# A chunked attention with an 8-expert layer behind it: q and k of six blocks loaded as two tokens per row, and the routing's sums moved to another engine

## The chip, the cores and the metric

One core of a Trainium2 chip. The metric is the device time of one execution in microseconds (us).

## What is computed

From q, k and v of shape (4 batches, 8 heads, 768 tokens, 64), 8 memory keys and values per batch and head, gate weights (512 x 8) and expert weights w1 (8 x 512 x 1024) and w2 (8 x 1024 x 512), all fp32:

```python
for c in range(768 // 32):                     # chunks of 32 queries
    k_ctx = k[:, :, max(0, 32*c - 16) : min(768, 32*c + 40)]   # 16 left, 8 right; v alike
    s = q_c @ concat(mem_k, k_ctx).T / 8
    a = exp(s - max(s)); out_c = (a / (sum(a) + 1e-9)) @ concat(mem_v, v_ctx)
x = out as (3072 tokens, 512)
P = exp(x @ w_gate - max)
for _ in range(8):                             # the routing
    P /= P.sum(1, keepdims=True) + 1e-9
    P /= P.sum(0, keepdims=True) + 1e-9
    P *= 3072 / 8
y = sum over the experts e of P[:, e:e+1] * (relu(x @ w1[e]) @ w2[e])
```

## The kernel before

All 8 experts work on all 3072 tokens, in units of 512 tokens (six per expert, 48 in all). Each fp32 operand of a large product is split into two f16 parts, high and low, and a product is three passes of TensorE over the parts (high x high, high x low, low x high). From the second expert on the products use a seven-product form of 2x2 blocks, with sums of operands formed ahead; the first expert's outputs use the plain form.

**Attention** runs in 24 blocks of 128 tokens, four to a unit, and is spread over the first units. For block n, `load_block` (L834) loads q as 128 tokens x 8 heads x 64 (256-byte runs in memory, L850) and k likewise, shifted left by 16 tokens (L844, L845, L847). `load_extra` (kx, L784 to L792) loads the k rows between blocks and the memory keys, once for four blocks. `transposed` turns q and k, two heads at a time, by products with the identity (tiles tq, L1008, and tk, L1012: four transposes 128x128 each; tx, L808, for kx), and ACT copies them into qT (L1036) and kC (L1016 to L1029). Scores go to sp (L1071, 64 small products), DVE takes maxima and differences (sm L1085, s L1091), ACT the exponent, PE turns it (ta, L1128), and the values' product is xp (L1138). DVE scales it (rec, xq) and turns it into xg. Values are loaded by L923, one piece of 56 KB at a time, on SP's queue and, for block 0, on ACT's too.

**Scales.** Before a tensor is split it is scaled by a power of two found from its largest element. For x of the first unit: vmax of blocks 0 and 1 (DVE, L976), most_of (L445), a product row_x (L494) that lays the 128 maxima in a row, a maximum, a product sp_x (L481) that spreads it, and ux and sx on DVE (L456, L457). For the first weights alike: mxs (L557), row_w, sp_w, uw and sw. Then ACT makes the high part and DVE the low part of x and w (L513, L521), and the first expert's first products start (pp, L2040).

**Routing** (L1458 to L1545) starts when all logits (lg, 128 x 24 x 8) are there, beside the fifth and sixth units of the first expert. Each of 8 iterations has on DVE a row sum rs (L1494), its reciprocal (L1495, L1496), the scaling of lg (L1497) and a column sum cs (L1501); on PE cp, a product with ones (L1529), which adds over the partitions; on DVE cr (L1510, L1511) and the scaling of lg (L1512).

**Low parts.** In a unit's hidden part, L1821 subtracts the high from the full sum (h<-ss,h, 128x1024). It runs on POOL for units n < `ASIDE` (1) and on DVE for the others. POOL otherwise forms weight sums (ws, L601), operand sums (xt) and collects outputs (acc, L1926).

**What sets the order.** Every step is given to a planner (class Plan, L85 to L240) with an engine, a cost, the steps it needs and a due time. It lays them out in time and emits each engine's instructions in that order; the engines then run in that order, each waiting only for what its next instruction needs. Due times hang on START and TURN (the planned start and length of the first unit), UNIT (36.7, the others), `begin(n)` and `needed(n)` (when block n's result is due). Where PE has over 0.4 us to wait by the plan, `pad` puts in fillers, tile warm (L427), products with the identity that nobody reads, a count worked out from the gap:

```python
n = int((at - now - 0.1) * 0.8 / 0.11)
```

Of the kernel before, what the change touches and what calls it, by code (L numbers as in the profile page):

```python
# [233 lines left out]
def tile_chunked_attn_sinkhorn_moe(  # L234
# [28 lines left out]
    P = 128  # L263
# [29 lines left out]
    small = ctx.enter_context(tc.tile_pool(name="small", bufs=1))  # L293
    xpool = ctx.enter_context(tc.tile_pool(name="xpool", bufs=1))
# [51 lines left out]
    START, TURN, UNIT, AHEAD = 28.2, 63.0, 36.7, 50.0  # L346
# [3 lines left out]
    ASIDE = 1  # L350
# [388 lines left out]
    def needed(n):  # L739

        if n < BU:
            return (11.0, 17.5, 36.0, 41.0)[n]
        return PACE + ((n + 1) / BU - 1.0) * AHEAD - 12.1

    state = {}
    extra = {}
# [86 lines left out]

    def load_block(n):  # L834
# [4 lines left out]
        qt = buf("q", att, [P, H, D], F32, f"q_{n}")  # L839
        kt = buf("k", att, [P, H, D], F32, f"k_{n}")  # L840

        def go_k():
            if blk == 0:
# [5 lines left out]
        lq = add(  # L849
            "SP", 1, lambda: nc.sync.dma_start(qt.t, rows(q, b, t0, QB)), (), at, [qt], dma=1.55  # L850
        )
        lk = add("SP", 2 if blk == 0 else 1, go_k, (), at + 0.1, [kt], dma=1.55)
# [142 lines left out]
    def transposed(n):  # L995
# [10 lines left out]
        def go_q():  # L1006
            for i in range(HP):
                nc.tensor.transpose(tq.t[:, i], flat(qt, i), ident)  # L1008

        def go_k():  # L1010
            for i in range(HP):
# [19 lines left out]
        t = add("PE", 0.5, go_q, [lq], at, [qt, qT], takes=tq)  # L1031
# [11 lines left out]
        t = add("PE", 0.5, go_k, [lk], at, [kt, kC], takes=tk)  # L1043
# [413 lines left out]

    def routing(deps):  # L1458
# [4 lines left out]
        urgent = begin(LATE) + 58.5  # L1463
# [27 lines left out]
        def rows(it):  # L1491
            def go():
                rs = small.tile([P, NT], F32, tag="rs", bufs=1, name=f"rs_{it}")
                nc.vector.tensor_reduce(rs, lg, axis=AX.X, op=ALU.add)  # L1494
                nc.vector.tensor_scalar_add(rs, rs, 1e-9)  # L1495
                nc.vector.reciprocal(rs, rs)  # L1496
                nc.vector.tensor_tensor(  # L1497
                    lg, lg, rs[:, :, None].broadcast_to([P, NT, E]), op=ALU.mult
                )
                box[it] = small.tile([P, E], F32, tag="cs", bufs=1, name=f"cs_{it}")  # L1500
                nc.vector.tensor_reduce(  # L1501
                    box[it], lg.rearrange("p t e -> p e t"), axis=AX.X, op=ALU.add
                )
# [3 lines left out]
        def columns(it, cp):  # L1507
            def go():
                cr = small.tile([P, E], F32, tag="cr", bufs=1, name=f"cr_{it}")
                nc.vector.tensor_scalar_add(cr, cp.t, 1e-9)  # L1510
                nc.vector.reciprocal(cr, cr)  # L1511
                nc.vector.scalar_tensor_tensor(  # L1512
                    lg,
                    lg,
                    float(N) / float(E),
                    cr[:, None, :].broadcast_to([P, NT, E]),
                    op0=ALU.mult,
                    op1=ALU.mult,
                )

            return go

        for it in range(8):
            t = add("DVE", 1.8, rows(it), [t], urgent)
# [3 lines left out]
                0.4,  # L1528
                lambda it=it, cp=cp: nc.tensor.matmul(  # L1529
                    cp.t, ones, box[it], start=True, stop=True  # L1530
                ),
                [t],
                urgent,
                takes=cp,
            )
            t = add("DVE", 0.8, columns(it, cp), [t], urgent, frees=cp)
# [786 lines left out]
```

## Time and profile before

| | us |
|---|---|
| median of 3 runs | 1913.08 (1911.89 to 1914.97) |
| the profiled execution | 1913.3 |
| its span | 1911.5 |
| PE busy in the span | 1898.8 (99%) |
| DVE, ACT, POOL busy | 1468.1, 1022.5, 503.0 |
| mean granted clock of TensorE | 0.999 of full |

The profile follows one execution. Starts are counted from the span's start. PE is the multiplication of TensorE and PEld its weight load; DVE is VectorE, ACT ScalarE, POOL GpSimd, SP the engine that issues most DMAs. A timeline row covers neighbouring instructions of one kind; what stands in brackets is the engine's idle time before it and what ended that. The granted clock is 1.00 at 2.4 GHz and 0.50 at 1.2 GHz.

### The profile page before, as it was taken

How to read it: one execution, taken by the hardware profiler on the slowest of the kernel's cores; microseconds unless marked ns; L12 is line 12 of the kernel's file. 1: busy time of each engine (PE TensorE's matmuls, PEld its weight loads, DVE VectorE, ACT ScalarE, POOL GpSimd, SP SyncE). 2: the span in 40 equal slices, each digit the busy share in tenths (PEclk: the TensorE clock that was granted, in tenths of full speed). 3: DMA queues.
4: the chain of work that ended last, by engine and by line, in shares of the span. 5: the costliest groups of instructions: out<-in, count | busy, mean ns of one | idle time of the engine just before them, and what ended most of it. 6: DMA issues, size and time to landing. Idle time of an engine off the chain costs nothing.

```text
span 1911.5 us, 47024 instructions
## 1 busy us (share of the span) xinstructions
PE 1898.8 (99%) x19535; PEld 1634.8 (86%) x19535; DVE 1468.1 (77%) x2456; ACT 1022.5 (53%) x1999; POOL 503.0 (26%) x541
## 2 busy tenths in 40 slices
PE   8999999999999999999999999999999999999999
PEld 7777676788888888888888888888888888888888
DVE  5887679878589867898668875898678885786565
ACT  4665555556465545546446544655555563564453
POOL 1210012514134211522224231342124232332112
PEclk9999999999999999999999999999999999999999
DMA  8787653543324432264224433245313632222321
GB/s 198 189 219 182 160 173 133 169 169 106 126 80 160 150 134 77 90 217 165 84 91 154 165 119 114 84 155 188 127 45 111 247 112 97 98 84 83 127 84 67
DMA packets 212998, 254.81 MB, mean 133 GB/s; under 512 B 112240, under 2 KB 146480, under 8 KB 208432
## 3 DMA queue, kind: packets, MB, share of 16 engines
q1 hardware_dynamic: 210660, 251.21, 40.4%
q8 instruction: 153, 2.51, 0.6%
q10 hardware_dynamic: 2124, 0.59, 0.2%
q14 instruction: 61, 0.50, 0.1%
HBM read 187.84 MB, written 63.44 MB: 131 GB/s over the span
## 4 chain that ended last, share of the span: by engine, by line
PE 97%; DVE 2%; SPq 0%; ACT 0%; issue 0%; DMA 0%; POOL 0%; DVEq 0%; POOLq 0%
PE px L1593 26%; PE yx L1593 23%; PE pz L1593 13%; PE yz L1593 11%; PE py L1593 6%; PE yp L2121 6%; PE yy L1593 6%; PE pp L2040 1%; PE xp L1138 1%; PE sp L1071 1%; PE warm L427 1%; DVE w L521 1%; PE ta L1128 1%; PE tk L1012 1%; PE tq L1008 1%; SPq L923 0%
## 5 line engine op out<-in xcount | busy, mean ns | idle before, releaser
L1593 PEld LDWEIGHTS <-w 128*128 128x128 f16 x7896 | 771.2, 98 | 94.4 <-issue 2.8
L1593 PEld LDWEIGHTS <-h 128*128 128x128 f16 x7056 | 690.4, 98 | 81.1 <-issue 0.9
L1593 PE MATMUL px<-x,w 128*128 128x256 f16 x4512 | 547.8, 273 | 1.5 <-DVE c L1662 1.0
L1926 POOL TENSOR_TENSOR acc<-acc,y 128x256 f32<-128x256 f32 x252 | 262.4, 1049 | 881.1 <-ACT y L1901 868.5
L1593 PE MATMUL yx<-w,h 128*128 128x256 f16 x4032 | 467.9, 273 | 0.5 <-DVE acc L1936 0.5
L1652 ACT ACTIVATE q<-px 128x256 f32<-128x256 f32 x376 | 143.1, 382 | 289.6 <-PE px L1593 285.1
L1593 PE MATMUL pz<-x,w 128*128 128x256 f16 x2256 | 278.1, 273 | 0.0
L1593 PE MATMUL yz<-w,h 128*128 128x256 f16 x2016 | 233.8, 273 | 0.0
L1821 DVE TENSOR_TENSOR h<-ss,h 128x1024 f16<-128x1024 f32 x168 | 217.6, 1298 | 3.3 <-ACT h L1797 3.3
L1772 ACT ACTIVATE h<-c 128x768 f16<-128x768 f32 x168 | 140.7, 838 | 112.2 <-DVE c L1662 112.2
L1797 ACT CAST h<-ss 128x1024 f16<-128x1024 f32 x168 | 174.2, 1040 | 39.5 <-DVE ss L1761 39.5
L1761 DVE SCALAR_TENSOR_TENSOR ss<-c,ss 128x256 f32<-128x256 f32 x336 | 176.6, 525 | 8.6
L1805 DVE SCALAR_TENSOR_TENSOR h<-c,h 128x768 f16<-128x768 f32 x168 | 168.7, 1007 | 9.2 <-ACT h L1772 9.1
L1662 DVE SCALAR_TENSOR_TENSOR c<-px,q 128x256 f32<-128x256 f32 x188 | 77.8, 421 | 94.8 <-PE px L1593 85.6
L1901 ACT ACTIVATE y<-yx,pscale 128x256 f32<-128x256 f32 x168 | 79.6, 474 | 120.5 <-PE yx L1593 116.5
L1593 PE MATMUL py<-x,w 128*128 128x256 f16 x1128 | 139.0, 273 | 0.0
L2121 PE MATMUL yp<-w,h 128*128 128x512 f16 x576 | 132.0, 379 | 0.9 <-DVE h L2082 0.9
L1761 DVE SCALAR_TENSOR_TENSOR ss<-c,h 128x512 f32<-128x512 f32 x168 | 125.6, 748 | 1.9 <-ACT h L1749 1.9
L1662 DVE SCALAR_TENSOR_TENSOR c<-py,q 128x256 f32<-128x256 f32 x188 | 78.5, 421 | 62.0 <-PE py L1593 58.7
L1593 PE MATMUL yy<-w,h 128*128 128x256 f16 x1008 | 116.9, 273 | 0.0
L2121 PEld LDWEIGHTS <-h 128*128 128x128 f16 x576 | 55.3, 99 | 60.0 <-DVE h L2082 1.4
L513 ACT ACTIVATE w<-ws,sw 128x1024 f16<-128x1024 f32 (+1 forms) x64 | 69.5, 1090 | 65.7 <-POOL ws L601 65.6
(155 smaller groups left out, 1739.6 us busy)
## 6 DMA issues: line engine op xcount, KB each, us to landing
x<-xkeep SPq DMA_DIRECT2D x28, 1792.0 KB
akeep<-acc SPq DMA_DIRECT2D x168, 256.0 KB
acc<-akeep SPq DMA_DIRECT2D x168, 256.0 KB
w1f<-in_moe_w_dram SPq DMA_DIRECT2D x36, 512.0 KB
w2f<-in_moe_w_dram SPq DMA_DIRECT2D x32, 512.0 KB
w1fm<-in_moe_w_dram SPq DMA_DIRECT2D x28, 512.0 KB
w2fm<-in_moe_w_dram SPq DMA_DIRECT2D x28, 512.0 KB
xkeep<-x SPq DMA_DIRECT2D x6, 1792.0 KB
```

The source lines that it names most:

```text
L513: lambda: nc.scalar.activation(dst(0), src(), AF.Copy, scale=s),
L1593: nc.tensor.matmul(dst.t, a, b, start=(not more and n == 0), stop=(n == end), skip_group_check=more,)
L1652: lambda: nc.scalar.activation(t.t, src.t, AF.Copy, scale=DOWN),
L1662: lambda: nc.vector.scalar_tensor_tensor(c.t[:, o], src.t, DOWN, q.t, op0=ALU.mult, op1=ALU.add),
L1761: lambda: nc.vector.scalar_tensor_tensor(dst(), src(), 0.0, other(), op0=ALU.max, op1=op),
L1772: lambda: nc.scalar.activation(h.t[:, 0, 0:3], c.t, AF.Relu),
L1797: lambda: nc.scalar.copy(h.t[:, 0, 3:7], ss.t),
L1805: lambda: nc.vector.scalar_tensor_tensor(h.t[:, 1, 0:3].rearrange("p a n -> p (a n)"), c.t.rearrange("p a n -> p (a n)"), 0.0, h.t[:, 0, 0 ...
L1821: lambda: spare.tensor_tensor(h.t[:, 1, 3:7], ss.t, h.t[:, 0, 3:7], op=ALU.subtract),
L1901: (lambda: nc.scalar.activation(t.t, src.t, AF.Copy, scale=f))
L1926: lambda: nc.gpsimd.tensor_tensor(acc.t[:, cols], acc.t[:, cols], q.t, op=ALU.add),
L2121: nc.tensor.matmul(py.t, hf.t[:, hl, where[fh], o : o + P], room(fp, WIDE * wl + DM * fh, WIDE * wl + DM * (fh + 1)), start=(fp == 0 and i ...
```

## The change

- **Rows of two tokens.** q and k of blocks 0 to 5 are loaded as 64 partitions x 8 heads x 128, with 512-byte runs, into one half of a room of 128 partitions (block n in half n % 2). From block 6 on they are loaded as before, into the same rooms; block 6 waits until block 5 is turned.
- **Turned by products.** `two_turns` replaces the four transposes of such a block by 16 products 64x64 with the identity, whose results go to every second column of tq or tk.
- **Routing.** The row sums, the scaling by rows, the column sums and the scaling by columns go to POOL, as chains of two-operand sums in a new tile, tree. DVE keeps the reciprocals. The step is due earlier (begin(LATE) + 30.0, not 58.5).
- **ASIDE** goes from 1 to NU + 2 = 8: the eight L1821 subtractions of the first two units with the seven-product form go from DVE to POOL.
- **Plan times** (START, TURN and the due times of a unit's rebuilding, of weights and of maxima) become other numbers.

```diff
-    START, TURN, UNIT, AHEAD = 28.2, 63.0, 36.7, 50.0
+    START, TURN, UNIT, AHEAD = 30.0, 66.0, 36.7, 50.0
...
-    ASIDE = 1
+    ASIDE = NU + 2
...
+    def twos(src, b, t, m):
+
+        return src[b, :, t : t + m].rearrange("h (p a) d -> p h (a d)", a=2)
+
+    def two_turns(to, t, n):
+
+        r = slice(n % 2 * HB, (n % 2 + 1) * HB)
+        for i in range(HP):
+            for a in range(2):
+                for par in range(2):
+                    nc.tensor.matmul(
+                        to.t[par * D : (par + 1) * D, i, a::2],
+                        t.t[:, 2 * i + par, a * D : (a + 1) * D],
+                        ident[r, r],
...
+        cost = 1.1 if n < TWOS else 1.55
+
+        def go_q():
+            nc.sync.dma_start(qt.t, twos(q, b, t0, QB) if n < TWOS else rows(q, b, t0, QB))
...
+            if n < TWOS:
+                return two_turns(tq, qt, n)
             for i in range(HP):
                 nc.tensor.transpose(tq.t[:, i], flat(qt, i), ident)
...
-        urgent = begin(LATE) + 58.5
+        urgent = begin(LATE) + 30.0
...
+        def row_sums():
+            two = tree[0][:, 0 : NT * E // 2].rearrange("p (t e) -> p t e", t=NT)
+            one = tree[0][:, NT * E // 2 :].rearrange("p (t e) -> p t e", t=NT)
+            plus(two, lg[:, :, 0 : E // 2], lg[:, :, E // 2 :])
+            plus(one, two[:, :, 0:2], two[:, :, 2:4])
+            plus(rs, one[:, :, 0], one[:, :, 1])
...
+        def over_rows():
+            nc.gpsimd.tensor_tensor(
+                lg, lg, rr[:, :, None].broadcast_to([P, NT, E]), op=ALU.mult
+            )
...
+            plus(a, lg[:, 0 : NT // 2], lg[:, NT // 2 :])
+            plus(b, a[:, 0:6], a[:, 6:12])
+            plus(a[:, 0:3], b[:, 0:3], b[:, 3:6])
+            plus(a[:, 3], a[:, 0], a[:, 1])
+            plus(a[:, 4], a[:, 3], a[:, 2])
...
-            t = add("DVE", 1.8, rows(it), [t], urgent)
+            t = add("POOL", 1.0, row_sums, [t, opened[0]], urgent)
+            t = add("DVE", 0.5, row_parts, [t], urgent - 300.0)
+            t = add("POOL", 2.1, over_rows, [t], urgent)
...
-            t = add("DVE", 0.8, columns(it, cp), [t], urgent, frees=cp)
+            t = add("DVE", 0.5, column_parts(cp), [t], urgent - 300.0, frees=cp)
+            t = add("POOL", 0.8, over_columns, [t], urgent)
...
-                    rebuild(u, begin(n) - 12.5)
+                    rebuild(u, begin(n) - 20.0)
...
-                weights(0, fp, 1, begin(1) - 16.8 + 2.0 * fp)
-            maxima(1, begin(3) + 15.8)
+                weights(0, fp, 1, begin(1) - 10.0 + 2.0 * fp)
+            maxima(1, begin(3))
...
-                weights(e + 1, fp, 1, begin(n + 1) - 8.9 + (0, 0, 20.0, 24.0)[fp])
+                weights(e + 1, fp, 1, begin(n + 1) - 4.0 + (0, 0, 20.0, 24.0)[fp])
```

How the new plan orders the instructions is seen at three places. The first is PE between the spreading of x's scale (sp_x) and the first pp. Before:

```order
L494 MATMUL row_x_619<-ident,most_of 1x128
L494 MATMUL row_w_0_625<-ident,most_of 1x128
L1012 MATMUL tk_628<-ident,k_469 128x128 x4
L481 MATMUL sp_x_636<-most_of,one 128x1
L427 LDWEIGHTS ident
L427 MATMUL warm<-ident 128x256
...
L481 MATMUL sp_w_0_646<-most_of,one 128x1
```

and with the change:

```order
L482 MATMUL sp_x_671<-most_of,one 128x1
L495 MATMUL row_w_0_674<-ident,most_of 1x128
L1120 MATMUL sp_680<-kC,qT_639 32x64 x32
L482 MATMUL sp_w_0_721<-most_of,one 128x1
L428 LDWEIGHTS ident
L428 MATMUL warm<-ident 128x256
...
L861 MATMUL tq_727<-ident,q_room 64x64 x16
L861 MATMUL tk_750<-ident,k_room 64x64 x16
```

Behind the first piece 35 fillers follow and then the first pp; behind the second 12. The scores of block 2 and the turns of block 3, which stood behind the first pp, now stand ahead of it, and row_x stands earlier still, ahead of the second ta. In all PE's order has 183 fillers before and 134 now; ahead of the first pp they are 177 and 123. The turns ahead of it were those of three blocks and are those of four. From the sixth unit on PE's order is the same.

The second place is DVE ahead of x's low parts. Before:

```order
L456 TENSOR_SCALAR ux<-sp_x_636 128x1
L457 RECIPROCAL sx<-ux 128x1
L456 TENSOR_SCALAR uw<-sp_w_0_646 128x1
L457 RECIPROCAL sw<-uw 128x1
L976 TENSOR_REDUCE vmax<-w_0_2_357 128x1
L521 SCALAR_TENSOR_TENSOR x_648<-xg_466,sx,x_648 128x512 x2
```

and with the change:

```order
L457 TENSOR_SCALAR ux<-sp_x_671 128x1
L458 RECIPROCAL sx<-ux 128x1
L503 TENSOR_REDUCE most_of<-row_w_0_674 1x1
L451 TENSOR_SCALAR most_of<-most_of 1x1
L452 TENSOR_SCALAR most_of<-most_of 1x1
L1021 TENSOR_REDUCE vmax<-w_0_2_349 128x1
L457 TENSOR_SCALAR uw<-sp_w_0_721 128x1
L458 RECIPROCAL sw<-uw 128x1
L522 SCALAR_TENSOR_TENSOR x_714<-xg_510,sx,x_714 128x512 x2
```

The vmax of block 2's values (here in a tile named w) moved ahead of the weights' scale sw.

The third place is POOL in one iteration of the routing, where before it had none of it:

```order
L1581 TENSOR_TENSOR lg<-lg,column_parts 128x192
L1546 TENSOR_TENSOR tree<-lg 128x96
L1546 TENSOR_TENSOR tree<-tree 128x48
L1546 TENSOR_TENSOR row_parts<-tree 128x24
L602 TENSOR_TENSOR ws_1_0_5571<-w1f_0_5477 128x256
L1560 TENSOR_TENSOR lg<-lg,row_parts 128x192
L1546 TENSOR_TENSOR tree<-lg 128x96
L1546 TENSOR_TENSOR tree<-tree 128x48
L1546 TENSOR_TENSOR tree<-tree 128x24
L1546 TENSOR_TENSOR tree<-tree 128x8 x2
L602 TENSOR_TENSOR ws_1_0_5571<-ws_1_0_5571,w1f_0_5477 128x256
```

Between row_parts and the next row stands DVE's reciprocal, and behind the last tree stand PE's cp and DVE's column_parts; weight sums (ws) of other steps lie in between.

## Rows read from the trace of the kernel before

**Rows 1.** The page's first and fourth parts: busy time of each engine, and the chain by engine.

```profile
PE 1898.8 (99%) x19535; PEld 1634.8 (86%) x19535; DVE 1468.1 (77%) x2456; ACT 1022.5 (53%) x1999; POOL 503.0 (26%) x541
...
PE 97%; DVE 2%; SPq 0%; ACT 0%; issue 0%; DMA 0%; POOL 0%; DVEq 0%; POOLq 0%
```

**Rows 2.** Busy time of PE, PEld, DVE, ACT and POOL (and their instructions) in two long stretches of the span; then the granted clock, DMA's share and GB/s.

```profile
0.00:76.00 76.00, 69.45 (x1164) 52.49 (x1165) 54.40 (x102) 40.69 (x79) 15.15 (x21) 0.98 0.78 182
76.00:1908.00 1832.00, 1828.98 (x18371) 1582.19 (x18370) 1413.25 (x2355) 981.84 (x1921) 487.82 (x520) 1.00 0.40 131
```

**Rows 3.** PE's timeline up to the first pp: start, duration, line, operation, tiles, count, and the idle time before it with what ended it.

```profile
16.78 0.66 PE L1128 MATMUL ta<-ident,s 128*128 128x128 f32 x4 [0.57 <-ACT s L1110]
...
18.11 0.86 PE L1138 MATMUL xp<-v_pair,at 64*32 64x65 f32 x64 [0.19 <-ACT at L1147]
...
23.16 0.66 PE L1128 MATMUL ta<-ident,s 128*128 128x128 f32 x4 [0.72 <-ACT s L1110]
...
26.33 0.73 PE L1138 MATMUL xp<-v_pair,at 64*32 64x65 f32 x48 [1.49 <-DMA k<-in_k_dram]
26.99 4.68 PE L427 MATMUL warm<-ident 128*128 128x256 bf16 x26
31.51 0.60 PE L1008 MATMUL tq<-ident,q 128*128 128x128 f32 x4
...
34.53 4.00 PE L427 MATMUL warm<-ident 128*128 128x256 bf16 x35
38.37 0.82 PE L2040 MATMUL pp<-x,w 128*128 128x256 f16 x6
```

**Rows 4.** Two short stretches, columns as in rows 2: PE's busy time first, the granted clock third from the end.

```profile
25.00:26.00 1.00, 0.00 (x0) 0.00 (x0) 0.82 (x1) 0.00 (x0) 0.00 (x0) 1.00 0.54 121
28.00:31.00 3.00, 3.00 (x16) 2.14 (x15) 2.97 (x5) 0.00 (x0) 0.00 (x0) 0.50 0.48 106
```

**Rows 5.** PE's timeline behind the first pp: its two longest waits there, and the first output product of expert 1.

```profile
69.13 1.04 PE L2121 MATMUL yp<-w,h 128*128 128x512 f16 x4 [0.87 <-DVE h L2082]
70.88 0.66 PE L1012 MATMUL tk<-ident,k 128*128 128x128 f32 x4 [0.71 <-DVE lg L1425]
...
392.03 2.78 PE L1593 MATMUL yx<-w,h 128*128 128x256 f16 x24
```

**Rows 6.** The chain that ended last, in order of time: start, time from start to start, piece (a few matmul records are missing; sp has 64 products).

```profile
10.34 0.44 PE tk L1012 x4
...
11.98 0.39 PE tx L808 x4
...
13.56 0.80 PE sp L1071 x53
```

**Rows 7.** DVE's timeline around the first scales.

```profile
34.83 0.17 DVE L457 RECIPROCAL sw<-uw 128x1 f32<-128x1 f32 x1
35.24 1.22 DVE L976 TENSOR_REDUCE vmax<-w 128x1 f32<-128x1024 f32 x1 [0.24 <-DMA w<-in_v_dram]
36.38 1.41 DVE L521 SCALAR_TENSOR_TENSOR x<-xg,sx,x 128x512 f16<-128x512 f32 x2
37.70 2.73 DVE L521 SCALAR_TENSOR_TENSOR w<-w1f,sw,w 128x512 f16<-128x512 f32 x4
```

**Rows 8.** SP's timeline: DMA issues of v of block 0 and of k and v of block 2, with the time each group took to issue.

```profile
7.63 2.76 SPq L923 DMA_DIRECT2D v_pair<-in_v_dram  x5
...
19.31 3.53 SPq L847 DMA_DIRECT2D k<-in_k_dram  x1
22.93 7.54 SPq L923 DMA_DIRECT2D w<-in_v_dram  x8
```

**Rows 9.** POOL's timeline: a small memset, the first copy, which waits for v of block 0, and a weight sum beside the routing.

```profile
1.61 0.13 POOL L940 MEMSET x_room<- 128x16 f32 x1
12.78 2.05 POOL L915 COPY w<-v_pair 128x1040 f32<-128x1040 f32 x2 [11.04 <-DMA v_pair<-in_v_dram]
...
300.27 0.73 POOL L601 TENSOR_TENSOR ws<-w1f 128x256 f32<-128x256 f32 x1 [5.74 <-DMA w1f<-in_moe_w_dram]
```

**Rows 10.** Three stretches of 5 us and the 40 us of the routing, columns as in rows 2.

```profile
15.00:20.00 5.00, 4.24 (x152) 3.43 (x149) 2.88 (x7) 2.87 (x6) 1.83 (x2) 1.00 0.93 217
20.00:25.00 5.00, 3.99 (x60) 2.94 (x45) 4.93 (x8) 1.49 (x3) 0.00 (x0) 1.00 1.05 314
25.00:30.00 5.00, 3.67 (x65) 2.84 (x66) 3.55 (x7) 0.00 (x0) 0.00 (x0) 0.76 0.42 94
300.00:340.00 40.00, 40.00 (x281) 27.25 (x280) 37.38 (x101) 19.19 (x37) 7.96 (x11) 1.00 0.40 139
```

**Rows 11.** DVE's timeline: the small operations of one routing iteration, and the first low-part subtraction of expert 1's first unit.

```profile
303.38 0.16 DVE L1510 TENSOR_SCALAR cr<-cp 128x8 f32<-128x8 f32 x1
303.57 0.20 DVE L1511 RECIPROCAL cr<-cr 128x8 f32<-128x8 f32 x1
...
304.59 0.18 DVE L1495 TENSOR_SCALAR rs<-rs 128x24 f32<-128x24 f32 x1
304.80 0.30 DVE L1496 RECIPROCAL rs<-rs 128x24 f32<-128x24 f32 x1
...
361.07 1.75 DVE L1821 TENSOR_TENSOR h<-ss,h 128x1024 f16<-128x1024 f32 x1
```

**Rows 12.** POOL's instructions by line, the largest group: busy time, mean ns of one, idle time before.

```profile
L1926 POOL TENSOR_TENSOR acc<-acc,y 128x256 f32<-128x256 f32 x252 | 262.4, 1049 | 881.1 <-ACT y L1901 868.5 <-DMA acc<-akeep 10.0
```

More of the change, by code (lines that the diff above doesn't have):

```diff
@@ L293, in tile_chunked_attn_sinkhorn_moe @@
     small = ctx.enter_context(tc.tile_pool(name="small", bufs=1))
+    tree = []
     xpool = ctx.enter_context(tc.tile_pool(name="xpool", bufs=1))
@@ L832, in flat, with qk_buf, make @@
         return t.t[r, 2 * i : 2 * i + 2].rearrange("p h d -> p (h d)")
+    TWOS = 6
+    HB = QB // 2
+    qk_rooms = {kind: att.tile([P, 2 * H * D], F32, name=f"{kind}_room") for kind in "qk"}
+    def qk_buf(kind, n):
+        room_ = qk_rooms[kind]
+        def make(i):
+            if n < TWOS:
+                return room_[i * HB : (i + 1) * HB].rearrange("p (h d) -> p h d", h=H)
+            return room_[:, i * H * D : (i + 1) * H * D].rearrange("p (h d) -> p h d", h=H)
+        return rings[kind].take(make)
+    def twos(src, b, t, m):
[9 more added lines that the diff above has]
+                        ident[r, r],
+                        start=True,
+                        stop=True,
+                    )
     def load_block(n):
@@ L847, in go_k @@
                 nc.sync.dma_start(kt.t, rows(k, b, t0 - LC, P))
[L849 to L852, printed above, removed]
+        lq = add("SP", 1, go_q, out_q, at, [qt], dma=cost)
+        lk = add("SP", 2 if blk == 0 else 1, go_k, out_k, at + 0.1, [kt], dma=cost)
         state[n] = (qt, kt, lq, lk)
@@ L1029, in memory @@
             nc.scalar.copy(kC.t[:, :, :, WIN:KW], src.broadcast_to([P, HP, CB, NM]))
-        t = add("PE", 0.5, go_q, [lq], at, [qt, qT], takes=tq)
+        t = done_q[n] = add("PE", 0.85 if n < TWOS else 0.5, go_q, [lq], at, [qt, qT], takes=tq)
         done = [
@@ L1042, in transposed @@
         ]
-        t = add("PE", 0.5, go_k, [lk], at, [kt, kC], takes=tk)
+        t = done_k[n] = add("PE", 0.85 if n < TWOS else 0.5, go_k, [lk], at, [kt, kC], takes=tk)
         done.append(add("ACT", 0.8, windows, [t], at, [kC], frees=tk))
@@ L1456, in attention @@
         values(*pend.pop(0))
+    halves_at = small.tile([P, 2, NT], F32, name="row_parts")
+    cols_at = small.tile([P, E], F32, name="column_parts")
     def routing(deps):
@@ L1507, in columns @@
[L1507 to L1521, printed above, removed]
+        rs, rr = halves_at[:, 0], halves_at[:, 1]
@@ L1527, in routing @@
                 "PE",
-                0.4,
-                lambda it=it, cp=cp: nc.tensor.matmul(
-                    cp.t, ones, box[it], start=True, stop=True
+                0.2,
+                lambda cp=cp: nc.tensor.matmul(
+                    cp.t,
+                    ones,
+                    tree[0][:, 4 * E : 5 * E],
+                    start=True,
+                    stop=True,
                 ),
                 [t],
-                urgent,
+                urgent - 300.0,
                 takes=cp,
             )
-            t = add("DVE", 0.8, columns(it, cp), [t], urgent, frees=cp)
+            t = add("DVE", 0.5, column_parts(cp), [t], urgent - 300.0, frees=cp)
+            t = add("POOL", 0.8, over_columns, [t], urgent)
         def finish():
@@ L2223, in turn @@
                 late["ss"] = ctx.enter_context(tc.tile_pool(name="sr", bufs=1, side="right"))
+                late["t"] = ctx.enter_context(tc.tile_pool(name="tr", bufs=1, side="right"))
+                tree.append(late["t"].tile([P, NT * E // 2 + NT * E // 4], F32, name="tree"))
                 for group in ("att", "two"):
```

49 lines of the change are left out of this document (33 added, 16 removed).

## Prediction

> **What bounds it now.** I read the page's shares first: PE is busy for 1898.8 of 1911.5 us and is 97% of the chain [rows 1]. So the time falls only where PE gets less work, waits less, or runs at its full clock. Two long windows say where that can be: PE is idle for 6.55 us in the first 76 us and for 3.02 us in the 1832 us behind them [rows 2]. A change of loads and order can therefore gain in the first 76 us and hardly anywhere else; behind them it can only keep PE busy or lose.
>
> PE's timeline up to the first pp at 38.37 us [rows 3] shows three losses. The fillers (warm, which compute nothing) are the first: by PE's order 177 of 183 stand ahead of that pp. The second are waits of 0.57, 0.19, 0.72 and 1.49 us, together 2.97. The third is the clock: PE did nothing from 25 to 26 us, and from 28 to 31 us the granted clock was 0.50, the 1.2 GHz level [rows 4]. There 26 fillers took 4.52 us (26.99 to 31.51), 174 ns each, where 35 took 3.84 us (34.53 to 38.37), 110 ns each, at full clock [rows 3]; the half clock cost 26 x 0.064 = 1.7 us. Behind the first pp, waits of 0.87 and 0.71 us are the longest [rows 5].
>
> **Fillers.** PE's order has 49 fewer: 54 fewer ahead of the first pp, 5 more behind. 49 x 0.110 = -5.4 us. They go because the plan now expects work sooner; whether the gap they filled goes too is the question below.
>
> **Turns.** Twelve turns of four 128x128 transposes become sixteen 64x64 products. Four transposes take 0.44 us from start to start, the 64 score products 0.80, and four tx products, which use 64 rows and all 128 columns of the array, 0.39 [rows 6]. The new products use 64 rows and 64 columns each, pairs in the two column halves. By the tx row that is 8 pairs x 0.0975 = 0.78 if halves run side by side, and 16 x 0.0975 = 1.56 if not; by the score row, which keeps the whole array full with twice the products' area, 0.80. No row shows a result written to every second column of PSUM. Bounds 0.44 (nothing changes) and 1.56; I take 0.80, nearest the score row, whose small products also alternate halves. 12 x 0.36 = +4.3 us. The Trainium skill, "SBUF — State Buffer", section on the port swizzle (Door 1), says of PSUM in its hint on cachelines that a non-contiguous access pattern "significantly slows down matmuls"; the sum by that would be rival 3's. The trace of before holds no such write.
>
> **PE's own row** ahead of the first pp: -54 x 0.110 = -5.9; six turns dearer, 6 x 0.36 = +2.2; the turns of block 3, new there, 2 x 0.80 = +1.6; the scores of block 2, also new there, +0.8. Together -1.4. Behind it: those scores and turns are done (-0.80 - 0.88), four turns dearer (+1.4), five fillers (+0.55): +0.3. Sum of PE work over the kernel: **-1.1 us**.
>
> **DVE's row.** pp also needs the parts of x and w. Before, vmax of block 2 stands behind sw and starts at 35.24 with 0.24 idle put down to v's DMA; x's low parts follow at 36.38, w's at 37.70 [rows 7]. Now vmax of block 2 stands ahead of sw. If v of block 2 lands only at 35.2, then vmax (1.22) ends at 36.4, uw and sw at 36.8, x's low parts (1.41) at 38.2: w's start 0.5 us later than before. If it lands 2.4 us behind its last issue (30.47), as block 0's did (issued by 10.39, [rows 8]; its copy on POOL from 12.78, [rows 9]), that is at 32.9 and w's low parts start at 35.9, 1.8 us earlier. PE's own row, -1.4, lies between -1.8 and +0.5, so I take it for the first pp (37.0 us) and leave waits and clock as they are: the gaps that lose fillers become waits of about the same end.
>
> **Loads.** 256 KB of q came in 256-byte runs. The five microseconds from 15, with many such runs, show 217 GB/s at 0.93 share, those from 20, with w1's long rows, 314 [rows 10]: 1.2 us a load now, 0.84 at best. Six loads lie ahead of block 2's v, so DMA could be free some 2 us sooner. But while the issues of k and v of block 2 took 3.53 and 7.54 us [rows 8], DMA's share fell to 0.42 (25 to 30 us, [rows 10]); something other than volume held the end. I count 0 and keep -2 as an end.
>
> **Routing.** PE was busy without a gap from 300 to 340 us, where the iterations lie [rows 10], so taking sums off DVE gains PE nothing. It can lose: DVE now stops in its order at row_parts and column_parts until POOL has delivered, and the c results that PE's banks need stand behind them. Per iteration POOL has ten operations over 736 columns in all. A 128x256 sum takes 0.73 us [rows 9]: 736/256 x 0.73 = 2.1 us if only columns count, 7.3 if each costs as much. A 128x16 memset takes 0.13 us [rows 9], so some 0.1 is fixed; I take 2.1 + 1.0 = 3.1, nearest the low end, since eight of the ten have 96 columns or fewer. DVE's five small ones take 0.18 + 0.30 + 0.16 + 0.20 + 0.16 = 1.0, cp 0.3, one ws operation in between 0.73, and two entries into DVE's row half of a 1.2 us operation each [rows 7, 9, 11]: 6.3 us. Between two cp the new order has 6.5 to 8.5 us of PE work (60 to 78 products at the 110 ns of [rows 3]), 7.3 in the mean. I count 0, with ends 0 and +22 (POOL 7.3, chain 10.5, seven gaps).
>
> **The rest.** Eight low-part subtractions go from DVE to POOL, 2.9 to 4.2 us each as four 128x256 sums of 0.73 or 1.05 [rows 9, 12]; the first was done at 362.8 us [rows 11] and its products start at 392 [rows 5], which hides them. If that cover were gone they would cost 3 us each. Later due times for w's parts and maxima move DVE and ACT work behind other work; all unit and expert borders behind 76 us hold 3.0 us of PE idle [rows 2]. 0, ends -1 and +2.
>
> **Sum.** The profiled execution took 1913.3 us, 0.2 above the median of 1913.08; I apply -1.1 to the median: **1912.0 us**. What a measurement can tell from no change is about 0.2%, 3.8 us: faster means below 1909.3, slower above 1916.9.
>
> **Rivals.**
> 1. *The waits go too.* If v lands early and PE stays fed, the half clock (-1.7) and half the waits ahead of pp (-1.5) are gained on top: 1908.8, at best 1907. For it: the 1.49 us wait stood beside idle DMA and idle SP, and loads with half the packets may end that. Against: fewer fillers leave PE idle more, and idleness came ahead of the half clock.
> 2. *POOL's chain is late.* POOL's sums average 1049 ns beside a busy DVE [rows 12], 1.44 times 0.73: then POOL takes 4.5 us and the chain 8.0 with its ws sum, seven gaps lose 0.7 each: +4.9 - 1.1, 1916.9; from a chain of 7.3 us on it decides, and each further 0.5 costs 3.5. For: DVE is 93% busy there. Against: POOL only 20% [rows 10].
> 3. *The turns run one after another,* because writes to every second column hold up the next product. T = 1.56: 12 x 1.12 = 13.4 - 5.4 = +8.0: 1921; where a third of that hides in the 2.97 us of waits ahead of pp, 1918. For it: no row shows such writes. Against: the score products of alternate halves overlap [rows 6].
> 4. *The loads are no faster.* A load into 64 partitions may take what one into 128 does: v lands at 35.2, the first pp starts at 38.9, and with +0.3 behind it: 1913.9. The Trainium skill, "SBUF — State Buffer", section on the port swizzle (Door 1), states this: 64 partitions reach half of the ports, 196 against 328 GB/s. 256 KB at 196 would be an estimate of 1.34 us, the time of now. The trace of before holds no 64-partition load of that size.
>
> **Chances.** Forecast 0.35 (its own range 1909.5 to 1914.5), rival 1 0.28, rival 2 0.15, rival 3 0.08, rival 4 0.12, other losses 0.02. Faster takes rival 1 and the forecast's lower edge, 0.30; slower takes rivals 2 and 3 but for the mildest, and the rest, 0.24; the same, 0.46. The range that leaves 1 in 10 on each side is 1907.5 to 1919.0.
>
> **What the changed profile would show.** Right: a turn of 16 at about 0.8 us from start to start; the first pp at about 37 us; PE idle as before in the first 76 us; no PE wait from 295 to 345 us. Wrong: turns near 1.5 us; PE or DVE waiting for POOL's row_parts or tree; the first pp below 35 us with no 0.50 clock (rival 1) or behind 38.5 (rival 4). A wait of over 1 us behind 400 us would contradict my pricing of the plan times.

## The result and the profile after

The changed kernel takes 1930.68 us against 1913.08 for the kernel before, medians of three executions each: 1.0095 times as long, 95% interval 1.0078 to 1.0112, so 18 us slower. One execution of each, of 3532 and 2449 us, was in a slow state and is left out. The forecast was 1912.0 and its range ended at 1919.0. Below, a kernel's cost is its ratio to the kernel before times 1913 us, since several sets are compared. The profiled execution took 1929.3 us, span 1927.5.

The page's first and fourth parts, to be read against [rows 1]:

```profile
PE 1904.2 (99%) x19822; PEld 1637.7 (85%) x19822; DVE 1455.3 (76%) x2424; ACT 1022.3 (53%) x1999; POOL 561.6 (29%) x629
...
PE 92%; DVE 3%; POOL 2%; DMA 1%; issue 1%; SPq 0%; ACT 0%; ACTq 0%; POOLq 0%; DVEq 0%
```

PE still bounds the kernel, but POOL, DMA and issue stand in the chain where they stood at 0%. Windows say where; columns as in [rows 2]:

```profile
0.00:76.00 76.00, 67.01 (x1428) 52.95 (x1429) 50.11 (x94) 37.92 (x74) 12.16 (x17) 0.96 0.81 166
76.00:1924.00 1848.00, 1837.22 (x18395) 1584.80 (x18393) 1404.76 (x2331) 984.40 (x1927) 549.46 (x612) 1.00 0.40 131
28.00:34.00 6.00, 4.62 (x41) 3.16 (x43) 3.52 (x11) 0.00 (x0) 0.00 (x0) 0.50 0.64 113
300.00:340.00 40.00, 37.37 (x261) 25.12 (x260) 30.27 (x61) 21.22 (x39) 30.39 (x55) 1.00 0.36 132
358.00:362.00 4.00, 3.37 (x18) 2.47 (x19) 2.39 (x5) 1.36 (x5) 3.84 (x7) 0.63 0.00 0
```

PE is idle for 8.99 us in the first 76 (6.55 before) and for 10.78 behind them (3.02 before, [rows 2]). The six microseconds from 28 us run at the 0.50 clock, the 1.2 GHz level, where three did [rows 4]. In the 40 us of the routing, where PE had no gap [rows 10], it now has 2.63 us, and POOL is busy for 30.4 us instead of 8.0.

PE's timeline up to the first pp and at the first yx (start, duration, operation, idle before it). A fp32 product leaves two records, so a turn of 16 products stands as x32 (and the scores of a block, x64, are 32 products):

```profile
9.02 1.15 PE L861 MATMUL tq<-ident,q_room 64*64 64x64 f32 x32
10.00 1.10 PE L861 MATMUL tk<-ident,k_room 64*64 64x64 f32 x32
...
16.01 1.15 PE L861 MATMUL tq<-ident,q_room 64*64 64x64 f32 x32 [0.68 <-DMA q_room<-in_q_dram]
17.50 1.15 PE L861 MATMUL tk<-ident,k_room 64*64 64x64 f32 x32 [0.34 <-DMA k_room<-in_k_dram]
...
21.61 0.73 PE L1187 MATMUL xp<-v_pair,at 64*32 64x65 f32 x49 [0.97 <-issue]
...
29.39 0.47 PE L1187 MATMUL xp<-v_pair,at 64*32 64x65 f32 x13 [3.14 <-issue]
29.78 3.59 PE L428 MATMUL warm<-ident 128*128 128x256 bf16 x16
33.30 1.81 PE L861 MATMUL tq<-ident,q_room 64*64 64x64 f32 x32
...
42.01 2.24 PE L2109 MATMUL pp<-x,w 128*128 128x256 f16 x19
...
408.42 1.80 PE L1662 MATMUL yx<-w,h 128*128 128x256 f16 x15
```

A turn takes 9.02 to 10.00 = 0.98 us. Two 256 KB loads that PE waits for one behind the other land 17.50 - 16.01 = 1.49 us apart. The longest wait before pp is 3.14 us, and 16 fillers behind it take 3.52 us at half clock. The first pp comes 3.6 us later than before [rows 3], the first yx 16.4 later [rows 5]. From there to the end it is 1519.1 us against 1519.5: the whole loss lies before the first yx.

The routing's product cp on PE, five of its eight:

```profile
308.72 0.29 PE L1593 MATMUL cp<-tree,one 128*128 128x8 f32 x2
318.21 0.39 PE L1593 MATMUL cp<-tree,one 128*128 128x8 f32 x2 [0.67 <-POOL tree L1546]
327.25 0.39 PE L1593 MATMUL cp<-tree,one 128*128 128x8 f32 x2 [0.84 <-POOL tree L1546]
335.25 0.39 PE L1593 MATMUL cp<-tree,one 128*128 128x8 f32 x2 [1.12 <-POOL tree L1546]
...
358.63 0.39 PE L1593 MATMUL cp<-tree,one 128*128 128x8 f32 x2 [1.71 <-POOL tree L1546]
359.96 2.71 PE L1662 MATMUL py<-x,w 128*128 128x256 f16 x12
```

The eight stand 7.4 to 9.5 us apart, from 300.08 to 358.63: 8.36 in the mean. Five wait for POOL, together 4.9 us. Behind the longest the granted clock falls (0.63 in the mean from 358 to 362 us): the twelve py from 359.96 take 2.54 us to the next row's start, where twelve take 1.31 at full clock.

POOL in one iteration, and what DVE did beside it:

```profile
311.23 0.39 POOL L1546 TENSOR_TENSOR tree<-lg 128x96 f32<-128x96 f32 x1
311.70 0.27 POOL L1546 TENSOR_TENSOR tree<-tree 128x48 f32<-128x48 f32 x1
312.04 1.26 POOL L1546 TENSOR_TENSOR row_parts<-tree 128x24 f32<-128x24 f32 x1
313.26 0.73 POOL L602 TENSOR_TENSOR ws<-w1f 128x256 f32<-128x256 f32 x1
314.44 0.52 POOL L1560 TENSOR_TENSOR lg<-lg,row_parts 128x192 f32<-128x192 f32 x1 [0.45 <-DVE row_parts L1557]
315.04 1.30 POOL L1546 TENSOR_TENSOR tree<-lg 128x96 f32<-128x96 f32 x1
```

```profile
311.99 1.23 DVE L1789 SCALAR_TENSOR_TENSOR h<-c,h 128x1024 f16<-128x1024 f32 x1 [0.85 <-ACT h L1780]
313.34 0.69 DVE L1556 TENSOR_SCALAR row_parts<-row_parts 128x24 f32<-128x24 f32 x1
...
314.89 1.21 DVE L1789 SCALAR_TENSOR_TENSOR h<-c,h 128x1024 f16<-128x1024 f32 x1
```

A 128x96 sum takes 0.39 us alone and 1.30 when it falls under a DVE operation that reads two large tiles; a 128x24 sum, 0.23 to 0.29 alone, then takes 1.26. Its end comes with that operation's end or just behind: 313.30 and 313.22, 316.34 and 316.10. It goes the other way too: DVE's small operation on row_parts (L1556) takes 0.17 or 0.18 us in two of the eight iterations and 0.68 or 0.69 in the other six, each of these beside the 0.73 us weight sum that POOL starts there. POOL's two largest groups in the routing's window, by shape (count, busy time, mean ns):

```profile
L1546 POOL TENSOR_TENSOR tree<-lg 128x96 f32<-128x96 f32 x16 | 10.4, 651 | 22.4 <-ACT lg L1541 21.2
L1546 POOL TENSOR_TENSOR tree<-tree 128x48 f32<-128x48 f32 x16 | 8.7, 544 | 1.3
```

With five smaller groups (5.9, 5.1, 3.7, 3.1, 3.0) that is 39.9 us, 5.0 in each iteration; the prediction had 3.1.

### The profile page after: what moved, and what is told of

Its sections match the earlier page's. It is cut to its first block, busy times and chain, and to the rows that moved or that the text cites. A ratio compares the mean times of both kernels' runs of the same rounds, so it can differ in the third digit from the quotient of the medians.

```text
span 1927.5 us, 47645 instructions
## 1 busy us (share of the span) xinstructions
PE 1904.2 (99%) x19822; PEld 1637.7 (85%) x19822; DVE 1455.3 (76%) x2424; ACT 1022.3 (53%) x1999; POOL 561.6 (29%) x629
## 3 DMA queue, kind: packets, MB, share of 16 engines
q8 instruction: 155, 2.54, 0.6%
## 4 chain that ended last, share of the span: by engine, by line
PE 92%; DVE 3%; POOL 2%; DMA 1%; issue 1%; SPq 0%; ACT 0%; ACTq 0%; POOLq 0%; DVEq 0%
PE px L1662 25%; PE yx L1662 23%; PE pz L1662 12%; PE yz L1662 11%; PE py L1662 6%; PE yy L1662 6%; PE yp L2190 4%; POOL tree L1546 1%; PE xp L1187 1%; PE sp L1120 1%; PE pp L2109 1%; DMA v_pair<-in_v_dram 1%; DMA q_room<-in_q_dram 1%; PE ta L1177 1%; DVE w L522 1%
## 5 line engine op out<-in xcount | busy, mean ns | idle before, releaser
L1830 DVE SCALAR_TENSOR_TENSOR ss<-c,ss 128x256 f32<-128x256 f32 x336 | 170.3, 507 | 8.3
L1830 DVE SCALAR_TENSOR_TENSOR ss<-c,h 128x512 f32<-128x512 f32 x168 | 120.2, 715 | 2.8 <-ACT h L1818 2.7
```

The lines of the kernel that those rows point to most:

```text
L1830: lambda: nc.vector.scalar_tensor_tensor(dst(), src(), 0.0, other(), op0=ALU.max, op1=op),
```

## The experiments

Two theories stood at the start. By the first the loss is the **routing**, POOL's chain being longer than PE's work between two cp, and the rest is near zero. By the second it is the **rows of two tokens**, with dearer turns and slower loads. Each part alone came first.

**b_qk, b_routing, b_times: one part of the change each.** The kernel before with only the rows of two tokens and their turns; with only the routing on POOL and its due time; with only the plan times.

> The kernel before with one part of the change alone: q and k of six blocks in rows of two tokens, turned by products. Theory A (the loss ahead of 76 us is made by this part: turns of 0.98 us, 12 x 0.54 = +6.5, less 27 fillers x 0.11 = -3.0, and PE waiting at a border of its instruction fetch with a half clock behind it, +2 to +6): +5 to +10 us over before. Theory B (the plan times make that loss, and this part costs only its PE work): +3.5 us. The forecast's pricing (turns of 0.80, no new waits) would be +1.3 us.

> The kernel before with one part of the change alone: the routing's sums and scalings on POOL, due at begin(LATE) + 30. Theory A (POOL's chain is later than PE's row reaches cp: five waits of 4.9 us in all, a half clock behind the longest, 1.7 us, and longer cp): +6 to +9 us over before, with PE waiting for tree. Theory B (POOL's chain was late only because the turn and the start shifted everything): 0 to +2 us, no wait for tree over 0.3 us.

> The kernel before with one part of the change alone: the plan times (START, TURN and the five due times). It has 204 fillers where before has 183. Theory A (they cost next to nothing): -1 to +3 us, the 21 fillers being at most +2.3. Theory B (they make the loss ahead of 76 us, as sx, sw and the first pp are laid out otherwise): +4 to +8 us.

Measured: b_qk 1922.88, ratio 1.0048 [1.0031, 1.0065], +9.2 us; b_routing 1921.24, 1.0039 [1.0025, 1.0052], +7.5; b_times 1915.85, 1.0013 [1.0002, 1.0025], +2.5. They add up to 19.2 against 18.2 for all of it, so each theory holds about half. The eight low-part subtractions on POOL were not run alone; this sum leaves nothing for them, but each of its terms is uncertain by 2 to 3 us.

Where the time goes in the profiled executions: PE's busy and idle time up to the first yx, from where to the end of the span it is 1517 to 1519.5 us in all five.

| | first yx | PE busy before it | PE idle before it |
|---|---|---|---|
| the kernel before | 392.03 | 384.19 | 7.84 |
| b_qk | 401.11 | 389.17 | 11.94 |
| b_routing | 399.60 | 383.71 | 15.89 |
| b_times | 397.06 | 384.65 | 12.41 |
| the change | 408.42 | 390.55 | 17.87 |

What b_routing loses is idle time alone, 8.0 us more: 5.2 at cp, and the rest ahead of the routing, in waits for q and k (2.5) and on issue (2.7), where the kernel before has 1.5 and 1.2. In b_qk 5.0 us are PE's work, about what twelve turns (+6.5), 27 fillers less (-3.0) and 3.4 us more at half clock (some +1.7) make, and 4.1 are idle time; PE waits 4.4 us for q there.

**a_contig: turns that write neighbouring columns.** It changes the order of the tokens within a block.

```diff
-  to.t[par * D : (par + 1) * D, i, a::2],
+  to.t[par * D : (par + 1) * D, i, a * D : (a + 1) * D],
```

> The changed kernel, but each of the 16 turning products writes 64 neighbouring columns of PSUM in place of every second one; the tokens of a block then stand in another order, so the attention's numbers are not the reference's. Theory A (the turn's 0.98 us is the products' own time): a turn stays at 0.95 to 1.0 us and the time within 1 us of the changed kernel's 1931. Theory B (writes to every second column hold PE up): a turn falls to about 0.80 us, 12 x 0.18 = -2.2 us.

```profile
7.52 1.15 PE L861 MATMUL tq<-ident,q_room 64*64 64x64 f32 x32
8.50 1.10 PE L861 MATMUL tk<-ident,k_room 64*64 64x64 f32 x32
```

Still 0.98 us a turn, and 1928.1 us, 1.0079 [1.0061, 1.0097], 3 us under the change and within the uncertainty of both; so the time decides nothing between the theories, and the turn does. The stride costs nothing; 0.98 is the price of sixteen such products. Rival 3 as it was put falls. The Trainium skill's hint on cachelines ("SBUF — State Buffer", Door 1), that a non-contiguous pattern slows matmuls, does not show for this write.

**b_qk8 and b_qk4: old loads, in b_qk's order of instructions** but for four fillers. b_qk8 keeps products for the turn, eight of 128x64; b_qk4 goes back to the four transposes, so of the two-token part only the plan's order is left.

```diff
 b_qk8
-  nc.sync.dma_start(qt.t, twos(q, b, t0, QB) if n < TWOS else rows(q, b, t0, QB))
+  nc.sync.dma_start(qt.t, rows(q, b, t0, QB))
...
+  nc.tensor.matmul(to.t[par * D : (par + 1) * D, i], t.t[:, 2 * i + par], ident, ...
 b_qk4, on top
-  if n < TWOS:
-      return two_turns(tq, qt, n)
```

> As the run with the q and k part alone (its PE order is kept but for the turns), only that q and k are loaded as before (128 partitions, 256-byte runs) and a turn is 8 products of 128 rows x 64 columns. Theory A (loads into 64 partitions are no faster, rather slower, and PE's waits for q, 4.4 us there, and the half clock behind the longest come from them): the waits for q fall under 1.5 us and the time is 3 to 6 us under that run's 1922.9. Theory B (the turns and PE's instruction fetch make the loss, whatever the loads): within 2 us of 1922.9.

> As the run with old loads and turns of 8 products (0.93 us a turn, 1921.3 us), in the same PE order, but the twelve turns are the four transposes of before again (0.44 us). What is left of the q and k part is the order that the dearer turns and cheaper loads gave the plan. Theory A (PE's turns are on the path one for one): 12 x 0.49 = 5.9 us come off, 1914 to 1917, some 2 us over before. Theory B (the plan's order makes the loss; a shorter turn only lengthens the next wait): 1919 to 1921.

Measured: b_qk8 1921.29, 1.0046 [1.0034, 1.0058]; b_qk4 1924.54, 1.0056 [1.0043, 1.0070]. Old loads gain nothing: in b_qk8 the 4.4 us of waits for q are gone, and a wait of 3.62 us on issue stands at 24.61 in their place. Turns at the old 0.44 us gain nothing either, though 12 x 0.54 = 6.5 us of PE work are gone; b_qk4 lies above both theories. PE from 76 to 130 us in b_qk4, then in b_qk4_cost (below), then in the kernel before:

```profile
76.00:130.00 54.00, 47.55 (x847) 36.08 (x846) 43.43 (x75) 30.45 (x65) 13.47 (x17) 1.00 0.82 226
```

```profile
76.00:130.00 54.00, 51.91 (x941) 39.97 (x940) 42.59 (x79) 34.58 (x73) 14.01 (x17) 1.00 0.87 231
```

```profile
76.00:130.00 54.00, 53.69 (x1018) 41.91 (x1017) 42.96 (x83) 36.28 (x78) 12.70 (x17) 1.00 0.84 227
```

In b_qk4 PE is idle there for 6.45 us, 2.09 in b_qk4_cost, 0.31 in the kernel before. The saved work turned into waits: here for ACT's exponent (2.0 us) and on issue (2.0), and ahead of 76 us for loads of k (five waits, 3.3). A third theory followed: the **plan** is at fault. It books a two-token load at 1.1 us of DMA where it books the old one at 1.55, and lays steps out too early.

**b_qk4_cost, b_qk8_cost, b_qk_cost, b_qk_cost19: the planned cost of a load.** The same three kernels with the old 1.55, and b_qk with 1.9.

```diff
-  cost = 1.1 if n < TWOS else 1.55
+  cost = 1.55
```

> As the run with old loads and old transposes in the q and k part's order (1924.5 us), only that the plan counts 1.55 of DMA time for each of these loads again and not 1.1. Theory A (the loss is the plan's: it takes twelve loads for 0.45 us shorter than they are, 5.4 us in all, so PE's row meets attention products whose data are not there, 6.5 us of idle between 76 and 130 us): that idle falls under 2 us and the time is 1912 to 1917. Theory B (the order that the dearer turns gave makes it): 1920 or more.

> Old loads, planned at 1.55, with turns of 8 products (0.93 us) in place of the transposes; PE's order is that of the run with old loads and transposes at 1.55 (1913.5 us) and, but for four fillers and a few places, that of the q and k part at 1.55 (1925.6 us). Theory A (the loads into 64 partitions are slower, 1.49 against 1.2 us for 256 KB, and make most of what the mended plan leaves): 1914 to 1919, the turns' 12 x 0.49 = 5.9 us being the most that they can add; the loads are then the other 6 us or more. Theory B (the turns make it): 1922 to 1926.

> The kernel before with the q and k part alone (1922.9 us), only that the plan counts 1.55 and not 1.1 of DMA time for each of its loads. Theory A (as beside it): what stays is PE's own work, 12 x 0.54 less 10 fillers x 0.11 = +5.4 us over before, so 1916 to 1920. Theory B: 1921 to 1924.

> The q and k part alone, with its loads planned at 1.9 in place of 1.55 or 1.1 (1.55 x 1.49 / 1.2). It has 205 fillers. Theory A (what is lost is lost to a plan that takes the loads for too short): 1916 to 1921, under the 1925.6 at 1.55. Theory B (slower loads and dearer turns cost their time in any order): 1922 to 1926.

| turns | loads | planned 1.1 | planned 1.55 | 1.9 |
|---|---|---|---|---|
| 4 transposes | 128 partitions | 1.0056 | 1.0004 [0.9995, 1.0012], 1913.50 us | |
| 8 products | 128 partitions | 1.0046 | 1.0031 [1.0021, 1.0041], 1920.10 | |
| 16 products | 64 partitions | 1.0048 | 1.0068 [1.0054, 1.0082], 1925.61 | 1.0060 [1.0047, 1.0073], 1926.36 |

The first row is the plan's: one number, which changes only the order and the count of fillers (160 and 177), is worth 9.9 us; up to the first yx PE is idle for 18.9 us in b_qk4 and for 10.6 in b_qk4_cost. Down the column of 1.55, where the plan fits the loads of the first two rows, the parts show apart. Turns of 0.93 in place of 0.44 us cost (1.0031 - 1.0004) x 1913 = 5.2 us, and 12 x 0.49 = 5.9 was to be expected: in an order that fits, PE's own work is time (b_qk4_cost is as its theory A had it, b_qk8_cost between its two). In their profiled executions PE is busy for 8.0 us more in b_qk8_cost up to the first yx, part of it at half clock, and idle for 1.5 more. With the 64-partition loads and turns 0.05 dearer the kernel stands another 7.1 us higher, 0.6 of it the turns, above both theories; a planned 1.9 brings back 1.5, within the uncertainty of some 3. That the loads cost this is not shown by any row. The profiled execution of b_qk_cost is the shortest of its six (1917.30, the others 1923.61 to 1926.72), and PE waits only 1.0 us for q and k in it; b_qk_cost19, profiled at 1927.73, waits 0.5 us for them and 4.8 on issue. So with a plan that is too fast 9 to 11 us are lost whatever the parts cost, and with 1.55 it is 6 us with the dearer turns and 13 with the loads too. The plan's theory holds for the order as it is, that of the turns for an order that fits; what the loads cost in such an order stays open.

The loads themselves, in b_qk4 with 128 partitions: two waits of PE one behind the other.

```profile
32.87 0.66 PE L1051 MATMUL tq<-ident,q_room 128*128 128x128 f32 x4 [0.87 <-DMA q_room<-in_q_dram]
34.12 0.66 PE L1055 MATMUL tk<-ident,k_room 128*128 128x128 f32 x4 [0.59 <-DMA k_room<-in_k_dram]
```

1.25 us between landings against 1.49 with 64 partitions: 210 and 176 GB/s. Another such pair in b_qk4, from 27.48 to 28.64, stands 1.16 apart; with 64 partitions a_old_routing has 1.48 and b_qk_cost 1.49. The pairs lie at different places with other transfers beside them, and one of 128 partitions in b_routing stands 2.12 apart, so this is no clean price. In these pairs rows twice as long in half as many partitions are no faster, rather slower.

**a_old_routing: the change with the routing back on DVE** and its old due time.

> The changed kernel with the routing back on DVE as before, at its old due time; everything else as changed. Theory A (the parts add): the routing part's 8.0 us comes off, 1922 to 1925, and PE waits nowhere between 295 and 400 us. Theory B (the late start of the changed kernel hides part of the routing's loss): 3 to 5 us come off, 1926 to 1929.

Measured 1919.86, 1.0044 [1.0029, 1.0058]: 9.8 us less than the change. PE is busy without a gap from 300 to 370 us and the first yx stands at 396.14. Added to the kernel before, the routing costs 7.5 us; taken from the change, it gives back 9.8, more than either theory had.

**b_routing_cost and a_cost: POOL's planned costs.** POOL's three steps are booked at about what they took (1.0, 2.1 and 0.8 become 1.5, 3.4 and 1.0; DVE's 0.5 becomes 0.8); a_cost is the whole change with these and with loads at 1.55.

> The run with the routing part alone, with the planner's costs of its steps raised to what they took: POOL 1.0, 2.1, 0.8 to 1.5, 3.4, 1.0 and DVE's 0.5 to 0.8. The instructions are the same; only the places of cp in PE's order move back. Theory A (the loss is PE arriving at cp ahead of POOL's chain, which has time until the first products of the second expert read its result): PE's waits for tree fall under 1 us and the time is -1 to +2 us against before. Theory B (POOL's work itself slows DVE and so PE): +5 us or more remains.

> The changed kernel with its plan's costs as the chip showed them: loads 1.55, and the routing's steps on POOL 1.5, 3.4 and 1.0, on DVE 0.8. Nothing else. Theory A (orders laid out with costs that are too low make most of the 18 us): waits for tree under 1 us, 1917 to 1923. Theory B (the work itself): 1926 or more.

Measured: b_routing_cost 1916.66, 1.0021 [1.0012, 1.0030]; a_cost 1922.60, 1.0054 [1.0041, 1.0066], 7.8 us less than the change, at the upper end of theory A; b_routing_cost, +4.0 us, lies between its two theories. PE's waits by what they waited for (sum, times, longest), of b_routing and of b_routing_cost:

```profile
PE cp L1593 <- POOL tree L1546: 5.2, 7, 1.4
```

```profile
PE cp L1593 <- POOL tree L1546: 1.0, 3, 0.4
```

The cp now stand 9.0 to 10.9 us apart with more of PE's work between them, and 4.2 of the 5.2 us of waits are gone; the time falls by 3.4 us. So most of the routing's loss was PE's order holding a cp too early for a chain planned too short. Some 4 us stay. In this kernel's profiled execution (1913.15 us, the shortest of its 12) the first yx comes at 392.20, as before, so no row shows where they go.

**b_wide and a_wide: half as many fillers, twice as wide,** in the kernel before and in the change. PE's waits put down to issue come at the same counts of its records whatever the instruction there is (behind 348 or 349 matmul records in seven of the kernels, behind 476 in eight; the wait before xp in [rows 3] is one of the first kind, though its row names k); fewer, longer fillers (`two` has 512 columns) move that count to another place in the work.

```diff
-  for _ in range(n):
-      nc.tensor.matmul(wp, idle[:, 0:P], idle, start=True, stop=True)
+  for _ in range(n // 2):
+      nc.tensor.matmul(wp, idle[:, 0:P], two, start=True, stop=True)
```

> The kernel before with every two fillers of 256 columns made one of 512: the same PE time in half as many instructions, so each later instruction stands some 50 instructions earlier in PE's stream when xp of block 1 is reached. Theory A (the wait of 1.49 us in that xp is PE fetching its next instructions behind the data DMAs; such waits stand at every 127th recorded product, from 348 on, in all runs so far): no wait there; it goes to the 349th recorded product, which is now about a microsecond of work later, behind the time when that fetch landed, and the first pp comes 1.5 to 4 us earlier: 1909 to 1911. Theory B (it is a wait for k's load): xp still waits until about 26.3 us, the time stays within 1.5 us of before.

> The changed kernel with every two fillers of 256 columns made one of 512, as was done to the kernel before. Theory A (its wait of 3.1 us in block 1's xp, at the 476th recorded product, is PE's instruction fetch behind DMA's data, and the half clock follows from it): the waits move to other products (still the 349th and 476th recorded ones), and if these are reached when DMA has caught up the first pp comes 2 to 5 us sooner than 42.0: 1926 to 1930. Theory B (that xp waits for data): it waits until about 29.4 us again, 1930 to 1932.

Measured: b_wide 1912.25, 0.9995 [0.9986, 1.0003]; a_wide 1931.33, 1.0096 [1.0082, 1.0110]. In b_wide the wait of 1.49 us before xp [rows 3] is gone and so is the half clock:

```profile
23.73 0.86 PE L1141 MATMUL xp<-v_pair,at 64*32 64x65 f32 x64
...
35.04 0.82 PE L2043 MATMUL pp<-x,w 128*128 128x256 f16 x6
```

The first pp comes 3.3 us sooner than before, yet the time is the same: theory A's wait is gone, and theory B's time stands. By the first yx, at 390.73, 1.3 us of the gain are left; another wait on issue, of 2.58 us, stands at 119.41. In a_wide the 3.14 us wait leaves xp and a wait of 2.45 us stands ahead of a tq (at 32.22), so nothing is won.

What these waits are shows in DMA's rows. Of the changed kernel's page, the queue of instructions (packets, MB, share):

```profile
q8 instruction: 155, 2.54, 0.6%
```

155 packets of 16.4 KB; PE and PEld have 2 x 19,822 = 39,644 recorded instructions, 256 for each packet, and the later of these waits stand about 127 matmul records apart. In the change one packet starts at 26.40 us, takes 1.47, and PE goes on at 29.39, 1.5 us behind its end. In the kernel before one starts at 23.97 and takes 0.94; PE goes on 1.4 us behind it at 26.33. In b_qk8 it is 22.30, 0.93 and then 24.61, again 1.4; in a_wide 29.59, 1.18 and 32.22, 1.5. So PE was out of instructions until the next block had come. DMA's share was 1.0 to 1.3 while these packets of the change, the kernel before and b_qk8 were under way; why they did not start sooner no run shows. The Trainium skill, "Runtime: NRT & Kernel Launch", section on instruction fetch mechanics, states blocks of 16 KiB, 256 instructions, fetched by a DMA queue of the sequencer's own; the counts agree. It also calls the cost of such a block's border mostly hidden; these waits are not.

## Why the prediction was wrong, point by point

Two steps failed: to "leave waits and clock as they are" ahead of the first pp, and to count the routing as 0. Up to the first yx PE is idle for 17.9 us where it was for 7.8, and 3.4 us more run at half clock at the start and 3.4 in the routing. The routing makes 7.5 to 9.8 us of the loss, the rows of two tokens with the order that they gave the plan 9.2.

- **What bounds it: right, but for the places.** PE bounds it, and behind 76 us the change could only lose. It lost 7.8 us of PE idle there.
- **Routing, counted 0: wrong, and the largest single term.** Ten POOL operations were priced by columns and a fixed part from rows without disturbance: 3.1 us, and the sum of the undisturbed durations is indeed 3.3. They took 5.0, because about ten of the eighty took over 1.1 us, as those shown above beside DVE's operations with two large inputs, and others 0.2 to 0.4 us more than alone. From cp to cp it became 8.4 us where PE had 7.7 of work (forecast 6.3 and 7.3). That is rival 2's mechanism with its decision point and the sign that it named, PE waiting for tree; its 4.5 us for POOL were 5.0, its price, +4.9, was 7.5 to 9.8 as measured. It left out that the wait of 1.71 us also costs clock (the 18 products behind it took 1.7 us more than at full clock), and that PE can come to wait ahead of the routing too, 2.8 us more in b_routing. Rival 2's argument against itself, POOL only 20% busy, was no argument: what counts is when DVE's operations fall.
- **The rule that bore on this** is not in the prediction. The Trainium skill, "SBUF — State Buffer", section "Who interferes with whom", states that DVE operations with two inputs in SBUF and GpSimd's reads exclude each other. The trace agrees: 0.39 alone, 1.30 under a 1.21 us operation.
- **Turns, priced 0.80: 0.98.** 12 x 0.54 = +6.5 instead of +4.3. Inside the bounds, and the products make it, not the stride. One reading under the price was wrong: a block's scores are 32 products of 64x32 that leave two records each, not 64, so their 0.80 us were for the same area of the array as a turn's, not for twice as much.
- **Loads, counted 0 with an end at -2: no run shows a gain.** 1.49 us a load where the sum had 0.84 to 1.2. Planned at 1.55 the kernel with them stands 5 to 6.5 us above the one with old loads, turns taken off, but no row shows that the loads make it. Rival 4, no faster loads, is right in that; it sized them as the old ones. The Trainium skill's rule for rival 4 ("SBUF — State Buffer", Door 1) agrees in direction with the pairs above, 176 against 210 GB/s; its 328 for 128 partitions does not show here.
- **Fillers, -5.4, and PE's own row, -1.1: the wrong kind of step.** In the order of the change, PE's sum of work does not set the time: b_qk4 had 6.5 us less of turns than b_qk and was no faster. Of the 49 fillers 34 come back when the loads are booked at 1.55 (a_cost has 168), so most went because the plan booked loads too short; that such time comes back as waits is seen in b_qk4, with 17 fillers fewer than b_qk4_cost and 8.3 us more idle. One planned cost was worth 9.9 us. I read the order's shifts from the plan, and took its expectation of earlier work as harmless, where it was the loss.
- **First pp at 37.0: 42.01.** The 3.14 us fetch wait and the half clock behind it (16 fillers and a tq, some 2.4 us over their full-clock time) are most of it. I read the like wait before (1.49, beside idle DMA) as one that the loads make; it was a fetch too. Still, pp is a poor milestone: b_wide moved it 3.3 us and the time not at all.
- **The rest, 0 with +2: about right.** The plan times cost 2.5 us (interval 0.4 to 4.8). The low-part subtractions on POOL (the first takes 2.89 us at 373.96) were not run alone; nothing past the first yx moved. The wait that I named as a sign against this pricing did come, 1.35 us at 407.11 for DVE's c; none of b_qk, b_routing and b_times has it, so no run shows whose it is.

**Still open:** the 4 us of the routing left once cp is placed well; why b_qk gains nothing, or loses, from the mended 1.55, and whether its loads cost anything there; what the low-part subtractions cost; and some 2 us of the 12.8 between pp and yx that neither idle time (7.9), the half clock in the routing (1.7) nor added work (about 1) accounts for.

## What to carry to other kernels

When a planner writes the order, a change to its costs is a change of its own: time it apart (the old kernel with only the new order), since in one of these kernels 9.9 us hung on one number that no instruction contains. Before moving small sums from DVE to POOL, price each POOL operation as its own duration or the rest of the two-input DVE operation it falls beside, and compare the chain with the work that PE has between its two ends. Longer runs into half the partitions need not be a faster load; look at the time between landings, not the length of a run. To find where a loss lies, compare PE's busy and idle time up to one fixed piece of work, here the first yx.

## What the runs showed of the hardware that was not expected

- PE runs out of instructions, mostly in the first 230 us, with waits of up to 3.7 us (b_qk8_cost). The four followed to their packets end 1.4 to 1.5 us behind a 16 KB instruction packet of 0.93 to 1.47 us; DMA's share was 1.0 to 1.3 under three of these packets.
- A POOL sum of 0.39 us takes 1.30 beside a DVE operation with two large inputs, and a DVE operation of 0.18 us takes 0.69 beside a POOL sum of 0.73.
- Sixteen fp32 products 64x64 with a PSUM stride of two take 0.98 us, as without it; eight of 128x64 take 0.93; four 128x128 transposes of the same data take 0.44.
- In an otherwise steady stretch, a PE wait of 1.71 us behind several of 0.5 to 1.1 was followed by the lower level of the clock.
